# VectorE's attention heads in free row groups, with a re-ordered start, in a transformer block on one core

## The chip, the cores and the metric

The kernel runs on one core of one Trainium2 chip, whose engines each work through an instruction stream of their own: TensorE (PE, matmuls), ScalarE (ACT, activations), VectorE (DVE), GpSimd (POOL) and SyncE (SP, which issues the DMA transfers). The metric is the device time of one execution in microseconds (us). Three runs of the kernel before took 921.13, 921.31 and 921.42 us; the median is 921.31 us.

## The reference

The block is a pre-layernorm attention block followed by a gated MLP, for 2048 tokens of width 640, with 32 heads of width 20 and an MLP width of 1728. All inputs are bf16.

```python
x   = A_x                                          # [1, 2048, 640]
qkv = (layernorm(x) @ wqkv) -> q, k, v             # 32 heads of width 20
p   = softmax(q @ k^T * 20 ** -0.5)                # per head, 2048 x 2048
h   = x + (p @ v, heads side by side) @ wo
n   = layernorm(h)
h2  = h + (gelu_tanh(n @ w_gate) * (n @ w_up)) @ w_down
```

## The kernel before

**Who computes the exponentials.** The scores of 32 heads are 32 x 2048 x 2048 numbers, and every one needs an exp. The scores are computed transposed, in tiles of 128 keys by up to 512 queries for one head. Heads are packed by four (index `j` = 0 to 3): head `j` of a group `g` has its 20 rows of K and Q in partitions 32j to 32j+20 (`kt_all`, `qt_all`), so four heads use four different row groups of the PE array, and matmuls of different `j` can run beside each other. Most tiles get their exp on ACT (`activation` with Exp, out of PSUM into the ring `pts`/`pts2`). A part gets it on DVE, by an evacuation to int16 (line 870) and six arithmetic instructions per two or four tiles (`d_exp`).

**Chunks, slots, units.** The queries are cut in seven chunks (`CHUNKS`: 512, 512, 256, 256, 256, 128, 128). A chunk has slots; a slot is one to four head groups, in all 32 slots, and its sum over keys is gathered in PSUM bank 6. Within a slot some quads (a quad is one block of keys for four heads) are taken out for DVE (`D_QUADS`), and their single tiles are listed in `dq` with the place in the stream from which each is due (lines 793 to 811). The other tiles are walked in order and cut in units (lines 813 to 832): 3 tiles, then 2 tiles, and so on, because a unit's scores stand in PSUM banks 0 to 2 or 3 to 4 (chunk 1 uses 3 to 5 as well). One ACT instruction does the exp of a whole unit: 128x1536 or 128x1024. A unit can carry one tile for DVE (`xd`), which is the next in `dq` when it is due. `unit()` issues the scores of its own tiles (line 935), then the tile for DVE by an operation of its own into bank 5 or 7, then the exp, then the products with V (`pv_op`) of quads that are complete. The plan has 703 units, 1776 tiles for ACT and 272 tiles for DVE.

**A planner writes the order.** Every operation is recorded with an engine, an assumed duration, a priority, its reads and writes and its PSUM banks. `Sched.schedule` (line 120) plays this out as a list schedule: each engine takes the ready operation of the best priority, and the result is one fixed order per engine, with semaphore waits. All engines then run their lists in order. A changed duration in a call of `op` thus changes no work, but the order of everything. The priorities are `P_QK` 0 (scores, exps), `P_PV` 1, `P_PRO` 1.5 (the start), `P_EPI` 2, `P_LN` 2.5, `P_BG` 3 (projections and MLP in the background). Nearly all recorded lambdas have line 354 (`I`), so groups of the profile are told apart by their tiles.

**The start.** x is loaded by four DMAs (`x0` to `x3`, 4 tiles of 128 rows each). The layernorm statistics are computed by DVE (`ln_stats`), for `x1` by ACT (`act_stats`); ACT takes the square roots (`sd`), DVE the reciprocals (`rs`) and applies them (L354, `rege<-rege,mu,rs`). PE transposes the rows (line 592), and ACT or DVE (`T_DVE`) evacuates them into `xnT` (lines 598, 601). K and Q of tile 0 (four heads plus) are projected in blocks `c` of 512 tokens (`proj_qk`, matmuls in line 649) and evacuated by ACT (line 682); SP copies the rows to their partitions. `kd` holds the largest |k| of each row over all keys; with `sel0` and |q| a matmul (line 770) gives an upper bound of each query's scores, which is added as one more row of Q (line 774) and keeps the exp in range. Only then can the first scores start. Ones in column 20 of each head of `v_all` give the softmax sums.

**K tiles 1 to 4** are projected during chunk 0 (`proj_k`, `proj_q`, `q_bound`), evacuated by DVE (line 685) and go through HBM (`k_rows`, `q_rows`, `bounds`) to their partitions.

**Behind a chunk** `epilogue` divides by the sums and `post` does the output projection, the layernorm, and the MLP in the background of the next chunk (lines 1107, 1153, 1164). ACT's Gelu and Sqrt need another table than Exp: in the stream, a batch of Gelu (on DVE's copies of the gate values, line 1142) stands between two table loads. In `post` of the last chunk, the tail, ACT takes Gelu straight from PSUM (line 1129).

Of the kernel before, what the change touches and what calls it, by code (L numbers as in the profile page):

```python
# [307 lines left out]
SIZES = (512, 512, 256, 256, 256, 128, 128)  # L308
CHUNKS = tuple((sum(SIZES[:i]), n) for i, n in enumerate(SIZES))
# [14 lines left out]
D_FIRST, D_PART = 2, 0.75  # L324
# [5 lines left out]
P_QK, P_PV, P_PRO, P_EPI, P_LN, P_BG = 0, 1, 1.5, 2, 2.5, 3  # L330


def bass_sequential_preLN__mha_block__glu_gated_geglu__prompt_kernel(
# [12 lines left out]
    with ExitStack() as es:  # L346
# [133 lines left out]
        op("act", I("activation", nm[:, 0:1], zer[:, 0:2].bitcast(FP32), ACT.Sqrt), 1.5, P_QK, reads=["zer"], writes=["nm0"])  # L480
# [4 lines left out]
        op("dve", I("memset", f32(kt_all[:, 1:4, :]), ones2), 2.9, P_QK, writes=["kf0"])  # L485
# [16 lines left out]
        for j in range(4):  # L502
# [3 lines left out]
              base=0, pattern=[[-1, 128]], channel_multiplier=1), "identf")  # L506
        for g in range(0, NG, 2):
            cst(I("memset", f32(qt_all[:, 3, g:g + 2, :]), 0.0), "qf3%d" % g, 512)
        pvb0 = Bank(6)
        op("dve", I("memset", PS[:, 512 * 6:512 * 7], 0.0), 0.6, P_QK, acq=[pvb0], rel=[pvb0])  # L510
        op("dve", I("memset", v_all[:, :, :, DH:DH + 1], 1.0), 0.6, P_QK, writes=["vones"])
# [19 lines left out]
        e_ops = []  # L531
        C_POOL, T_POOL, T_DVE = 0.9, (), (13, 15)
# [11 lines left out]
        def ln_rsqrt(t0, n, prio, table=False, sqrt=False):  # L544
# [15 lines left out]
            if sqrt:  # L560
                op("act", I("activation", sd16[:, t0:t0 + n], sd16[:, t0:t0 + n], ACT.Sqrt), 0.2, 1, reads=[ks], writes=[ks])
                v(I("reciprocal", y, sd16[:, t0:t0 + n]), [ks], rk)
                return
# [15 lines left out]
        def ln_apply(eng, src, dst, dkey, t, rkeys, prio, first=False):  # L579
# [5 lines left out]
            return op(eng, fn, 0.82 if eng == "act" else C_POOL if eng == POOL else c_dve(D, 0.46), prio,  # L585
# [43 lines left out]
        for t0 in (0, 4, 8, 12):  # L629
# [6 lines left out]
            for t in range(t0, t0 + 4):  # L636
                e_ops.append(ln_apply(POOL if t in T_POOL else "dve", x_sb[:, t, :], xn_p[:, t % 4, :], ("xnp", t % 4), t, [f"x{t // 4}"], P_PRO,
# [9 lines left out]
        def chain(bk, key, n, steps, reads, prio, acq=True, after=()):  # L647
            for k, (l, r) in enumerate(steps):
                yield op("pe", lambda eng, l=l, r=r, k=k: eng.matmul(  # L649
                    bank(bk, n), l, r, start=(k == 0), stop=(k == len(steps) - 1)),  # L650
                    c_mm(n), prio, mode="full", util=n / 2400.0, reads=reads, writes=[key], acq=[bk] if (k == 0 and acq) else [],
# [17 lines left out]
        def proj_qk(col, t, c, dst, dkey, banks, prio, evac, after=(), peak=None):  # L669
# [9 lines left out]
            if peak and c == 3:  # L679
                after = (top(lambda: bank(bk), key),)  # L680
# [7 lines left out]
            if peak and c < 3:  # L688
                w_readers.append(top(lambda: dst, dkey))

        def proj_k(t, banks, prio, evac="dve"):
            for c in range(4):
                src = k_un[t % 2][:, 512 * c:512 * c + 512]
                proj_qk(D, t, c, src, ("ku", t % 2, c), banks, prio, evac, after=e_ops if t == 1 else (), peak=t == 0)
# [8 lines left out]
                if t and c == 3:  # L703
                    c0 = 0
# [552 lines left out]
```

## Time and profile before

| | before |
|---|---|
| median of 3 runs | 921.31 us |
| the profiled execution, its own time | 921.06 us |
| its span, first to last instruction | 919.1 us |
| ACT busy | 877.0 us (95%) |
| PE busy | 846.4 us (92%) |
| DVE busy | 794.5 us (86%) |
| exps on ACT | 370 of 128x1536, 333 of 128x1024 |
| first exp starts | 35.42 us |
| last exp ends | 883.5 us |

Times in the profile are counted from the start of the span. "Busy" is the union of the recorded instructions of an engine; instructions of one engine overlap in their records, since the next starts while the last one drains, so the step from start to start tells more than the recorded length. "Idle" in brackets names who released an instruction after a wait. The granted TensorE clock is 1.000 in this execution.

### The profile page before, as it was taken

Reading aid. Unit: us, or ns where it says so; the run is one execution under the profiler, and the core shown is the slowest. Engines: PE = TensorE matmul, PEld = TensorE weight load, DVE = VectorE, ACT = ScalarE, POOL = GpSimd, SP = SyncE. Lnnn points to the kernel's source line nnn. Section 1 sums busy time; section 2 is a strip of 40 time slices with the busy share of each in tenths; the row PEclk is TensorE's granted clock in tenths of the full one; section 3 lists DMA queues with packets and bytes.
Section 4 is the critical chain, followed back from the end, with each engine's and each line's share of the span. In section 5 each row is a group of like instructions: output and inputs, shape, how many; then the busy total and the mean of one; then the engine's idle time right before and its main releaser. Section 6 shows DMA issues by size and latency. Waiting matters only on the chain.

```text
span 919.1 us, 23058 instructions
## 1 busy us (share of the span) xinstructions
PE 846.4 (92%) x10159; PEld 355.6 (39%) x10159; DVE 794.5 (86%) x1456; ACT 877.0 (95%) x787; POOL 42.1 (5%) x121
## 2 busy tenths in 40 slices
PE   3999999999898987989998998999999999999998
PEld 1432323222232222223343333344444445666577
DVE  7779999999799996988888999899999988878763
ACT  6899999999999999999999999999999999999961
POOL 5000000000001000000001000000202000100200
PEclk9999999999999999999999999999999999999999
DMA  7211021234701000000111000010110001000000
GB/s 257 82 33 44 19 55 50 80 77 89 274 1 30 1 1 2 1 1 16 44 30 31 2 2 1 1 17 30 23 37 2 16 9 38 17 17 24 9 17 16
DMA packets 39516, 34.36 MB, mean 37 GB/s; under 512 B 19436, under 2 KB 36936, under 8 KB 39416
## 3 DMA queue, kind: packets, MB, share of 16 engines
q1 hardware_dynamic: 39416, 32.89, 12.9%
q8 instruction: 80, 1.31, 0.6%
q14 instruction: 20, 0.16, 0.1%
HBM read 20.12 MB, written 8.09 MB: 31 GB/s over the span
## 4 chain that ended last, share of the span: by engine, by line
ACT 62%; PE 27%; DVE 11%; issue 1%; DVEq 0%
ACT pts L354 39%; ACT rege L354 22%; PE ps L935 8%; PE ps L1107 6%; PE ps L354 5%; DVE qt_all L354 4%; PE ps L1164 4%; PE ps L649 3%; DVE qt_all L870 2%; ACT L354 1%; DVE rege L870 1%; DVE stats L354 1%; PE ps L592 1%; PE ps L1030 1%; DVE rege L354 1%
## 5 line engine op out<-in xcount | busy, mean ns | idle before, releaser
L354 ACT ACTIVATE pts<-ps 128x1536 bf16<-128x1536 f32 (+1 forms) x471 | 559.3, 1318 | 3.5 <-PE ps L935 1.5
L935 PE MATMUL ps<-qt_all,kt_all 32*128 32x256 bf16 (+2 forms) x3584 | 320.8, 288 | 37.7 <-ACT pts L354 22.3
L354 ACT ACTIVATE rege<-ps 128x1536 bf16<-128x1536 f32 (+1 forms) x232 | 285.2, 1317 | 2.6 <-PE ps L354 2.0
L935 PEld LDWEIGHTS ps<-qt_all,kt_all 32*128 32x128 bf16 x3584 | 104.3, 92 | 259.0 <-ACT pts L354 135.1
L354 DVE TENSOR_TENSOR qt_all<-qt_all 128x2048 f16<-128x2048 f16 (+3 forms) x186 | 174.9, 940 | 2.2
L1107 PE MATMUL ps<-rege,regw 128*128 128x256 bf16 (+2 forms) x980 | 160.9, 290 | 9.9 <-ACT rege L354 3.4
L354 PE MATMUL ps<-pts,v_all 128*21 128x256 bf16 (+2 forms) x2080 | 122.6, 290 | 0.0
L870 DVE TENSOR_SCALAR qt_all<-ps 128x512 int16<-128x512 f32 x128 | 87.6, 685 | 27.5 <-PE ps L935 27.0
L870 DVE TENSOR_SCALAR rege<-ps 128x512 int16<-128x512 f32 x128 | 87.5, 684 | 15.6 <-PE ps L935 13.9
L1107 PEld LDWEIGHTS ps<-rege,regw 128*128 128x128 bf16 x980 | 71.9, 97 | 70.6 <-issue 28.7
L354 PE MATMUL ps<-rege,v_all 128*21 128x256 bf16 (+2 forms) x1204 | 94.9, 295 | 0.3
L649 PE MATMUL ps<-regw 128*128 128x512 bf16 (+1 forms) x360 | 87.9, 353 | 1.1 <-DVE rege L870 0.6
L354 DVE TENSOR_SCALAR qt_all<-qt_all 128x1024 f16<-128x1024 int16 (+2 forms) x153 | 84.9, 559 | 1.8
L1164 PE MATMUL ps<-regw,rege 128*128 128x320 bf16 x448 | 79.0, 301 | 1.7 <-DVE rege L1153 0.6
L354 DVE TENSOR_TENSOR rege<-rege 128x1024 f16<-128x1024 f16 (+4 forms) x102 | 66.0, 657 | 1.0
L354 PE MATMUL ps<-kt_all,zer 128*32 128x512 bf16 x736 | 60.6, 384 | 0.0
L354 PEld LDWEIGHTS ps<-pts,v_all 128*21 128x21 bf16 x2080 | 44.9, 91 | 33.3 <-issue 29.3
L354 DVE TENSOR_SCALAR rege<-rege 128x1024 int16<-128x1024 int16 (+2 forms) x117 | 50.2, 447 | 1.1
L1164 PEld LDWEIGHTS ps<-regw,rege 128*128 128x128 bf16 x448 | 37.3, 97 | 33.9 <-issue 16.2
L1153 DVE TENSOR_TENSOR rege<-rege,ps 128x512 bf16<-128x512 bf16 (+1 forms) x53 | 35.7, 676 | 14.3 <-PE ps L1107 14.1
L649 PEld LDWEIGHTS ps<-regw 128*128 128x128 bf16 x360 | 29.2, 98 | 46.8 <-issue 24.8
L354 PEld LDWEIGHTS ps<-rege,v_all 128*21 128x21 bf16 x1204 | 32.4, 91 | 24.7 <-issue 16.8
(106 smaller groups left out, 564.9 us busy)
## 6 DMA issues: line engine op xcount, KB each, us to landing
rege<-in_A_x_dram SPq DMA_DIRECT2D x6, 640.0 KB, 5.2
q_rows<-regw SPq DMA_DIRECT2D x20, 128.0 KB, 1.7
out_dram<-rege SPq DMA_DIRECT2D x16, 160.0 KB, 1.8
regw<-in_B_w_gate_dram SPq DMA_DIRECT2D x1, 2160.0 KB, 12.8
regw<-in_B_w_up_dram SPq DMA_DIRECT2D x1, 2160.0 KB, 17.8
regw<-in_B_w_down_dram SPq DMA_DIRECT2D x1, 2080.0 KB, 22.9
kt_all<-k_rows SPq DMA_DIRECT2D x12, 160.0 KB
qt_all<-q_rows SPq DMA_DIRECT2D x12, 160.0 KB
```

What stands on the lines that cost most here:

```text
L354: return lambda eng: getattr(eng, method)(*args, **kwargs)
L592: op("pe", lambda eng, a=a: eng.transpose(bank16(bk, D)[:, 128 * a:128 * a + 128], src[:, a * 128:(a + 1) * 128], ident[:]), 0.055, prio, ...
L649: yield op("pe", lambda eng, l=l, r=r, k=k: eng.matmul(bank(bk, n), l, r, start=(k == 0), stop=(k == len(steps) - 1)), c_mm(n), prio, mode ...
L870: d_ops.append(op("dve", lambda eng: eng.tensor_scalar(v[:, 512 * h:512 * h + 512], bank(b), EXP_MUL, -32000.0, ALU.mult, ALU.max), c_dve( ...
L935: return lambda eng: eng.matmul(out()[:, kk * nq:(kk + 1) * nq], kt_all[32 * j:32 * j + 32, g, kt * 128:(kt + 1) * 128], qt_all[32 * j:32 ...
L1030: op("pe", lambda eng, tt=tt: eng.transpose(bank(b2)[:, tt * 128:(tt + 1) * 128], osb[:, s, tt * 128:(tt + 1) * 128], identf[:]), c_mm(128 ...
L1107: op("pe", lambda eng, a=a, f=f, fi=fi: eng.matmul(bank(bk)[:, fi * nq:(fi + 1) * nq], w[:, a, F0[f]:F0[f] + 128], hnT[:, a, 128 * tb:128 ...
L1153: hdone.append(op("dve", lambda eng, bu=bu, fv=fv, w=w: eng.tensor_tensor(fv, fv, bank(bu, w), ALU.mult), c_dve(w), p, reads=[ku] + hkeys( ...
L1164: op("pe", lambda eng, f=f, o=o, hf=hf, bk=bk: eng.matmul(bank(bk, 320), ha_f[:, o:o + 128], wd[:, f, hf * 320:(hf + 1) * 320], start=(f = ...
```

## The change

1. The memset of V's ones goes from DVE's list to POOL's, behind `identf`.
2. At the start, evacuations of K and Q wait for the three square roots that are still to come (`sqrts`); tile 11's transposes go to DVE's evacuations (`T_DVE`); the four DMAs of Q's tile 0 come ahead of K's by a better priority; `cold` adds 0.1 us to the planned duration of early matmuls; two more planned durations are raised.
3. The largest |k| of K tiles 1 to 4 is found block by block with one `tensor_reduce` each, as for tile 0, in place of a mask, three maxima and a reduce over the whole tile. For tiles 1 to 4, Q is projected ahead of K.
4. A unit's tile for DVE is picked from the next four in `dq`, of the same quad, so that its `j` is none of the unit's own. If none fits, the unit carries none. The planned duration of its scores is 0.01 us (0.21 where `j` is shared) and was 0.08 us.
5. Planned durations of scores and of products with V are 0.222 us per unit or quad (0.215, 0.218), and chunk 0's tiles for DVE are spread over 0.65 of a slot (`D_PART`, 0.75).
6. `BASE`, `SIX`, `P_LND`, `P_LNP`, `q_done` write out what was computed or fixed before, with the same values.

```diff
-D_FIRST, D_PART = 2, 0.75
+D_FIRST, D_PART = 2, 0.65
...
-        op("dve", I("memset", f32(kt_all[:, 1:4, :]), ones2), 2.9, P_QK, writes=["kf0"])
+        op("dve", I("memset", f32(kt_all[:, 1:4, :]), ones2), 4.2, P_QK, writes=["kf0"])
...
+        cst(I("memset", v_all[:, :, :, DH:DH + 1], 1.0), "vones", 512)
         for g in range(0, NG, 2):
             cst(I("memset", f32(qt_all[:, 3, g:g + 2, :]), 0.0), "qf3%d" % g, 512)
...
-        op("dve", I("memset", v_all[:, :, :, DH:DH + 1], 1.0), 0.6, P_QK, writes=["vones"])
...
-        C_POOL, T_POOL, T_DVE = 0.9, (), (13, 15)
+        T_DVE = (11, 13, 15)
...
+            cold = 0.1 if prio == P_PRO and not any(("xnT", tt) in reads for tt in range(4, NT)) else 0.0
...
-                    c_mm(n), prio, mode="full", util=n / 2400.0, reads=reads, writes=[key], acq=[bk] if (k == 0 and acq) else [],
+                    c_mm(n) + cold, prio, mode="full", util=n / 2400.0, reads=reads, writes=[key], acq=[bk] if (k == 0 and acq) else [],
...
-            if peak and c == 3:
-                after = (top(lambda: bank(bk), key),)
+            if prio == P_PRO:
+                after = tuple(sqrts)
+            if peak and c == 3 and t == 0:
+                after += (top(lambda: bank(bk), key),)
...
-            if peak and c < 3:
+            if peak and (c < 3 or t):
                 w_readers.append(top(lambda: dst, dkey))
...
-                if t and c == 3:
-                    c0 = 0
-                    n = 2048
-                    w_readers.append(op("dve", I("tensor_scalar", ka[:, 512 * c0:512 * c + 512].bitcast(I16),
...
-            for n in (1024, 512, 256) if t else ():
-                op("dve", I("tensor_tensor", ka[:, 0:n], ka[:, 0:n], ka[:, n:2 * n], ALU.max), 0.066 + n * 0.00052, prio,
...
-                        [("qu", 0), "qtm0"], "qc", 2.2, prio)
+                        [("qu", 0), "qtm0"], "qc", 2.2, prio - 0.1)
...
-            if di < len(dq) and dq[di][0] <= i:
-                xd = dq[di][1]
-                di += 1
-            n = len(bs) - (1 if six and xd else 0)
+            n = len(bs)
+            if dq and dq[0][0] <= i:
+                n -= 1 if six else 0
+                js = [x[3] for x in tiles[i:i + n]]
+                q = dq[0][1][:3]
+                fit = [k for k in range(min(4, len(dq))) if dq[k][1][:3] == q and dq[k][1][3] not in js]
+                if fit:
+                    xd = dq.pop(fit[0])[1]
+                elif six:
+                    n += 1
...
-            qk = op("pe", fns, 0.215, P_QK, mode="row", util=0.0533 * len(al), reads=reads, writes=[("S", u), "qkseq"] + ([("SD", xd)] if six else []), acq=bks)
+            qk = op("pe", fns, 0.222, P_QK, mode="row", util=0.0533 * len(al), reads=reads, writes=[("S", u), "qkseq"] + ([("SD", xd)] if six else []), acq=bks)
...
-                qd = op("pe", [qk_mms(lambda: bank(bd), xd, kk) for kk in range(512 // CHUNKS[slots[xd[0]][0]][1])], 0.08,
+                qd = op("pe", [qk_mms(lambda: bank(bd), xd, kk) for kk in range(512 // CHUNKS[slots[xd[0]][0]][1])],
+                        0.21 if xd[3] in [x[3] for x in tl] else 0.01,
...
                     pr = P_EPI if t == 1 else P_BG
+                    proj_q(t, 0, BG0, pr)
                     proj_k(t, BG0, pr)
-                    proj_q(t, 0, BG0, pr)
```

## The prediction

> **What bounds the kernel.** I read the page first, then ScalarE's timeline, then all engines at the start, at the longest waits and in the tail. The page's busy row and its chain of waits:
>
> ```profile
> PE 846.4 (92%) x10159; PEld 355.6 (39%) x10159; DVE 794.5 (86%) x1456; ACT 877.0 (95%) x787; POOL 42.1 (5%) x121
> ACT 62%; PE 27%; DVE 11%; issue 1%; DVEq 0%
> L354 ACT ACTIVATE pts<-ps 128x1536 bf16<-128x1536 f32 (+1 forms) x471 | 559.3, 1318 | 3.5 <-PE ps L935 1.5 <-PE ps L354 1.4
> ```
>
> ACT carries the chain from 42 to 866 us, nearly all of it exps. The 370 wide exps step by 1.330 us at best and the 333 narrow ones by 0.903: 370 x 1.330 + 333 x 0.903 = 792.8 us. Their steps in the trace sum to 812.3. So 19.5 us of lateness lies between exps; 35.4 us lie before the first, 35.6 behind the last. The change can act on these three parts alone: as the two programs are built, both have 370 and 333 exps.
>
> **The start, before.** DVE and POOL, then ACT and DVE around the first K block:
>
> ```profile
> 2.76 3.98 POOL L354 MEMSET kt_all<- 128x1024 f32 x4
> 4.22 0.48 DVE L354 MEMSET ps<- 128x512 f32 x1
> 6.54 0.48 DVE L354 MEMSET v_all<- 128x512 bf16 x1 [1.84 <-issue]
> ...
> 20.91 0.60 ACT L682 ACTIVATE regw<-ps 128x512 bf16<-128x512 f32 x1 [2.41 <-PE ps L649]
> 21.41 0.38 ACT L354 ACTIVATE sd<-sd 128x4 bf16<-128x4 bf16 x3
> 22.18 0.60 ACT L682 ACTIVATE regw<-ps 128x512 bf16<-128x512 f32 x1 [0.39 <-PE ps L649]
> 22.67 0.76 ACT L788 ACTIVATE v_all<-ps 128x320 bf16<-128x320 f32 x2
> 23.90 6.07 ACT L598 ACTIVATE regw<-ps 128x640 bf16<-128x640 bf16 x10 [0.46 <-PE ps L592]
> 35.42 1.45 ACT L354 ACTIVATE pts<-ps 128x1536 bf16<-128x1536 f32 x1 [1.12 <-PE ps L935]
> ...
> 21.54 0.69 DVE L677 TENSOR_REDUCE kd<-regw 128x1 f32<-128x512 bf16 x1 [1.09 <-ACT regw L682]
> 22.14 0.23 DVE L354 RECIPROCAL rs<-sd 128x4 f32<-128x4 bf16 x2
> 22.83 2.94 DVE L354 TENSOR_SCALAR rege<-rege,mu,rs 128x640 bf16<-128x640 bf16 x8 [0.45 <-DVE rs L354]
> 31.69 0.68 DVE L677 TENSOR_REDUCE kd<-ps 128x1 f32<-128x512 f32 x1
> 32.28 0.69 DVE L685 CAST rege<-ps 128x512 bf16<-128x512 f32 x1
> ```
>
> The ones of V wait 1.84 us, until POOL's fourth memset is nearly over, and the first layernorm statistics stand behind them at 6.65, though x0 landed at 5.17. Later, DVE's reciprocals stand behind a 0.69 us reduce; so normalised rows come at 22.83, and ten evacuations of 0.6 us keep ACT until 29.97.
>
> **Term 1, the start.** (a) Without the memset, statistics start at 5.2 and end near 19.3 (20.45 before; one wait for x2 eats 0.5). This alone buys little: PE's four V matmuls wait for `wv`, landed at 16.96, so K's first block starts at 18.2 rather than 18.56. (b) The square roots run in ACT's idle 2.41 us, reciprocals come before the reduce, and rows 4 and on are normalised from about 20. Then PE is late: K and Q's first blocks are ten matmuls, 0.427 us each until about 21.1 and 0.213 after, so they end at 21.8, and in the new order transposes follow at once, where ten V matmuls stood. Q's evacuation ends near 22.4, and ACT's transposed rows run from there. (c) They are nine, DVE taking tile 11: 22.4 + 9 x 0.6 = 27.8, against 29.97. (d) Behind them ACT's list has K, V, K where K, K stood: +0.4. (e) The 0.69 us cast is out of the bound's chain: -0.6. Sum: -2.2 + 0.4 - 0.6 = -2.4; I take **-2.3**, the first exp at 33.1. Ends: -1.0 (only c and part of e) and -3.5 (b and c by the rows' earlier readiness).
>
> Moved past by this: SP issues Q's four DMAs (0.75 us each) after two of K's, so K's block 0 lands up to 3.0 us later than 25.94; the first scores want it at 33. POOL's four `qt_all` memsets and the tiny `mu` operations move back by V's memset (0.48 on DVE; POOL's 128x512 took 0.54); POOL's next customer there is `mu` at 19.8, and it was idle from 15.5. Cover gone, that is 0.5 us.
>
> The Trainium skill (SBUF — State Buffer, "Who interferes with whom") speaks of a lock: a DVE operation in a 2-port mode and a POOL operation exclude each other for a whole instruction, while on trn2 it names no memset among such operations. By it the ones on POOL may now hold up a layernorm `tensor_scalar` for one memset, and the 1.84 us would be no lock and might stay. In the rows, such operations took 0.61, 0.51 and 0.61 us beside POOL's memsets at 13.2 to 15.6 and about 0.37 a step alone; by the rule's strict reading (a) is gone, and the sum moves by 0.4 us at most, since (b) to (e) don't rest on it.
>
> **Term 2, heads in free row groups.** I walked the planning loop of both versions. Before, 171 of the 272 tiles for DVE share `j` with a tile of their unit; after, none does. What sharing costs:
>
> ```profile
> 140.50 0.61 PE L935 MATMUL ps<-qt_all,kt_all 32*128 32x512 bf16 x3
> 141.80 0.39 PE L935 MATMUL ps<-qt_all,kt_all 32*128 32x512 bf16 x3
> ...
> 169.32 2.37 ACT L354 ACTIVATE pts<-ps 128x1536 bf16<-128x1536 f32 x2 [1.35 <-PE ps L354]
> ```
>
> Three matmuls with a shared `j` took 0.61 us, three without 0.39. So PE gets 171 x 0.22 = 38 us back, out of 781 us busy between 35 and 870 (of 835). PE isn't the bound, so the worth is what ACT no longer waits. Nearly all lateness comes at a wide exp behind a narrow one, when PE has only 0.9 us. Wide exps whose preceding unit carried a shared tile start 63 ns late on average (112 of them); behind a free tile 24 (78), behind none 21 (175). Taking 63 to 24 gives 112 x 39 ns = **-4.4 us**. Ends: 0 (other work fills PE's queue at the same points) and -7.1 (all 112 x 63).
>
> **Term 3, ends of slots.** Three waits over 0.7 us stand out: 0.8 at 142, 1.5 at 168, 1.5 at 694, each just ahead of an `osb` copy, a slot's end, where the products of DVE's last tiles bunch in PE's list and hold up the ring that exps write. Two are in chunk 0, where the last DVE tile was 4 to 5 units from the end; with `D_PART` and the new picks it is 7 to 9 in all slots but slot 5 (4). I take half of these two: **-1.2**. Ends: -3.8 and, as new waits may come in an order that is new everywhere, +3.
>
> **Term 4, the tail.**
>
> ```profile
> 883.53 1.28 ACT L354 ACT_TABLE_LOAD   x1
> 887.84 0.70 ACT L598 ACTIVATE rege<-ps 128x640 bf16<-128x640 bf16 x1 [2.81 <-PE ps L592]
> 892.77 0.21 ACT L354 ACTIVATE sd<-sd 128x1 bf16<-128x1 bf16 x1 [4.22 <-DVE sd L354]
> 912.32 3.98 PE L1164 MATMUL ps<-regw,rege 128*128 128x320 bf16 x28 [0.59 <-DVE rege L1132]
> ```
>
> The new list has two more table loads (16, was 14): chunk 5's Gelu now comes ahead of O's evacuation. ACT then has 1.28 + 0.2 + 1.28 + 1.7 = 4.5 us to do where 4.3 us lay between 883.53 and 887.84; the next load of 1.28 falls in the 4.22 us wait. So +0.2 of 2.6. PE, which is busy throughout, has 30.7 us of columns behind the last scores (31.0 before), and one wait more for DVE (0.6, as the row at 912.32). I take **+0.3**; ends -0.5 and +2.6.
>
> **Edits at nothing.** The block-wise reduces: 4 x 0.68 + 0.15 = 2.88 us against 0.68 + 0.68 + 0.41 + 0.28 + 0.41 = 2.46 per K tile, +1.7 us in all, on a DVE with 25 us idle between 35 and 275. Their cover is the 8 us between the landing of K and bounds for groups 1 and 2 (52.6) and first use (about 60); Q ahead of K takes some 2 of it, the start moves both. Without cover each late us costs one. The written-out constants keep their values.
>
> **Sum.** -2.3 - 4.4 - 1.2 + 0.3 = -7.6. Against the profiled execution's 921.06 that is 913.5; the median is 0.25 above it, so **913.7 us**.
>
> **Rivals.**
> - *PE's relief is not ACT's.* The late exps after shared tiles may owe their wait to what stands behind them in PE's list; PE's busy 93% speaks for it, the 63 against 24 against it. Term 2 is 0: 918.1. Chance 0.14.
> - *DVE tiles bunch (other side).* Chunk 0's eight tiles per slot need 8 x 0.6 + 4 x 3.33 = 18.1 us of DVE, now due within 0.65 x 26 = 16.9 us (19.5 before), and DVE was busy 93.3 of 100 us from 100 to 200. If DVE falls behind, PE's in-order list stops at bank 5 or 7 or at the slot's last products, as at 169.32, by 1.35 us. It decides from six such new waits on (8.1 against 7.6); one at each of the 20 slots in chunks 0 to 3 and term 3 gone: 913.7 + 1.2 + 13.5 = 928. The five tile buffers and the 9 us left to each slot's end speak against it. Chance 0.13.
> - *The change does nothing where it counts:* the start gains 1.0 by its low end, the tail loses that; 921.3. Chance 0.04.
>
> **Numbers.** The likeliest has 0.69; its own range adds its terms' likelier ends: -3.5 - 6 - 2 - 0.3 gives 909.5, -1 - 2 + 0 + 1.5 gives 919.8. To leave out no more than 2 in 10, I take 908.5 to 920.0, which also holds the first rival. 0.2% (1.8 us) is about what a measurement here tells from no change. Faster 0.83 (likeliest and first rival), same 0.04, slower 0.13.
>
> **What would show it.** The first exp near 33.1, its statistics from 5.2 on; scores of unit and tile for DVE in one 0.39 us; exps' lateness near 14 us and no 63 against 24; no wait over 0.7 us before 243; the tail 35 to 36 us. Wrong: new waits of ACT for PE L354 or L936 at slots' ends, or oT's evacuation over 5 us behind the last exp.

## The result and the profile after

The changed kernel took 922.38 us (median of 22 executions, 920.48 to 926.52), the kernel before 921.22 (920.35 to 921.89, also 22). The ratio is 1.0016, 95% interval 1.0010 to 1.0022: within 0.2% of no change, on its slow side, where 913.7 was forecast.

One thing is needed to read these numbers. The kernel before is tight; the changed one spreads, and the spread goes with the granted TensorE clock: its mean was 1.000 in 2 of the 22 executions (920.48 and 920.67), 0.998 in 10 (median 921.91), 0.996 in 6, 0.994 in 3 (median 924.06) and 0.989 in 1 (926.52). The profiled execution took 921.85 us at 0.998. The kernel before has such executions too, though fewer and cheaper: of the 84 that were timed beside the experiments, 62 had 1.000 (median 921.06), 16 had 0.998 (921.54) and 6 had 0.996 (922.02). So the changed kernel's two executions at the full clock lie about 0.5 us below the 921.06 of the kernel before (two are few), and the 1.2 us by which it is slower in the median go with the clock. The other 7 us that miss the forecast are missing at the full clock too.

The page of the changed kernel, the lines that answer to those shown of before:

```profile
PE 837.6 (91%) x10145; PEld 353.1 (38%) x10145; DVE 798.5 (87%) x1456; ACT 878.4 (95%) x788; POOL 38.3 (4%) x122
ACT 67%; PE 24%; DVE 8%; DMA 1%; issue 1%; POOL 1%
L357 ACT ACTIVATE pts<-ps 128x1024 bf16<-128x1024 f32 (+1 forms) x472 | 563.7, 1354 | 8.0 <-PE ps L936 4.8
L936 PE MATMUL ps<-qt_all,kt_all 32*128 32x256 bf16 (+2 forms) x3584 | 306.7, 289 | 46.6 <-ACT pts L357 26.6
```

TensorE was relieved (846.4 to 837.6 us busy), ScalarE is bound as before, and the idle time ahead of its exps rose from 3.5 to 8.0 us in the costliest group. "Lateness" is counted below as in the prediction: the step from one exp to the next, less 1.330 us (wide) or 0.903 (narrow), without the five steps that hold a Gelu. So counted, the kernel before has 18.47 us of it, where the prediction has 19.5. "Rests" in the table is what the last exp takes beyond its best step.

| profiled execution, us | before | after | difference | forecast |
|---|---|---|---|---|
| first exp | 35.42 | 32.75 | -2.67 | -2.3 |
| lateness to 100 us | 1.29 | 3.19 | +1.90 | |
| lateness 100 to 200 | 3.42 | 6.12 | +2.70 | |
| lateness 200 to 500 | 5.62 | 3.81 | -1.81 | |
| lateness 500 to 700 | 5.43 | 5.42 | 0.0 | |
| lateness behind 700 | 2.70 | 4.36 | +1.66 | |
| all lateness | 18.47 | 22.90 | +4.43 | -5.6 |
| five Gelu gaps and rests | 36.82 | 36.86 | 0.0 | |
| behind the last exp | 35.59 | 34.58 | -1.01 | +0.3 |
| span | 919.10 | 919.89 | +0.79 | -7.6 |

The start and the tail did what was forecast or better. The lateness went the other way, and three places in the trace carry it.

**The seventh exp.** ScalarE's timeline around the first exps, changed kernel:

```profile
31.36 1.28 ACT L357 ACT_TABLE_LOAD   x1
32.75 4.62 ACT L357 ACTIVATE pts<-ps 128x1536 bf16<-128x1536 f32 x4
37.23 2.40 ACT L357 ACTIVATE rege<-ps 128x1536 bf16<-128x1536 f32 x2
42.27 3.71 ACT L357 ACTIVATE pts<-ps 128x1536 bf16<-128x1536 f32 x3 [2.63 <-PE ps L357]
```

and the kernel before, ScalarE, then TensorE:

```profile
42.36 4.62 ACT L354 ACTIVATE pts<-ps 128x1536 bf16<-128x1536 f32 x4
...
41.38 0.61 PE L354 MATMUL ps<-pts,v_all 128*21 128x512 bf16 x8
```

Six exps start 2.67 us earlier, and the seventh starts at 42.27 against 42.36. It writes slots of the ring `pts` that the first products with V must have read; these are TensorE's matmuls at 41.61 (41.38 before). What they stand behind, VectorE and TensorE of the changed kernel:

```profile
37.40 0.68 DVE L871 TENSOR_SCALAR rege<-ps 128x512 int16<-128x512 f32 x1
37.99 0.68 DVE L691 CAST rege<-ps 128x512 bf16<-128x512 f32 x1
38.94 1.29 DVE L871 TENSOR_SCALAR rege<-ps 128x512 int16<-128x512 f32 x2 [0.26 <-PE ps L936]
40.14 0.68 DVE L681 TENSOR_REDUCE kd<-rege 128x1 f32<-128x512 bf16 x1
40.73 0.42 DVE L357 TENSOR_SCALAR rege<-rege 128x1024 int16<-128x1024 int16 x1
41.07 0.49 DVE L783 CAST v_all<-ps 128x320 bf16<-128x320 f32 x1
...
41.30 0.39 PE L742 MATMUL ps<-regw,sel 128*32 128x512 bf16 x1
41.61 0.61 PE L357 MATMUL ps<-pts,v_all 128*21 128x512 bf16 x8
```

VectorE works, with one gap of 0.26 us, on K tile 1 (L691, L681) and on the first tiles of slot 0 (L871), and its cast of a V tile (L783) comes at 41.07. The products start 0.54 us behind it.

**The bounds of group 4.** ScalarE, SP's queue, then TensorE, changed kernel:

```profile
138.00 1.54 ACT L357 ACTIVATE pts<-ps 128x1536 bf16<-128x1536 f32 x1
143.37 3.28 ACT L357 ACTIVATE pts<-ps 128x1024 bf16<-128x1024 f32 x3 [3.83 <-PE ps L936]
...
130.82 1.43 SPq L357 DMA_DIRECT2D kt_all<-k_rows  x4
136.50 0.32 SPq L357 DMA_DIRECT2D bounds<-regw  x1
137.97 0.57 SPq L357 DMA_DIRECT2D qt_all<-bounds  x1
...
140.50 0.61 PE L357 MATMUL ps<-rege,v_all 128*21 128x512 bf16 x8
...
142.94 0.60 PE L936 MATMUL ps<-qt_all,kt_all 32*128 32x512 bf16 x5
```

SP's queue, kernel before:

```profile
129.29 0.33 SPq L354 DMA_DIRECT2D bounds<-regw  x1
...
130.76 0.57 SPq L354 DMA_DIRECT2D qt_all<-bounds  x1
```

The bounds are written 7.2 us later than before, and slot 4 needs them at 139: lateness 4.04 us. Not all of this is the transfer's: the bounds have landed by 139.82 in the trace, but slot 4's scores start at 142.94, as TensorE's fixed list has products with V, projections and transposes in between.

**A dip of the clock.** Stretches of the changed kernel (from and to in us; length; busy time and count of PE, PEld, DVE, ACT, POOL; granted clock; DMA share; GB/s):

```profile
664.00:666.00 2.00, 1.51 (x33) 0.91 (x30) 2.00 (x4) 2.00 (x3) 0.30 (x2) 1.00 0.00 0
666.00:669.00 3.00, 1.81 (x18) 0.64 (x15) 3.00 (x5) 3.00 (x4) 0.00 (x0) 1.00 0.02 5
669.00:671.00 2.00, 1.89 (x32) 0.93 (x32) 2.00 (x7) 2.00 (x3) 0.00 (x0) 0.53 0.00 0
671.00:672.50 1.50, 1.50 (x26) 0.42 (x18) 0.85 (x2) 0.64 (x2) 0.00 (x0) 0.50 0.20 40
672.50:675.00 2.50, 2.50 (x41) 1.04 (x33) 1.53 (x4) 2.19 (x3) 0.00 (x0) 0.99 0.54 107
```

Behind a stretch in which TensorE had little but scores of 32 rows, the clock was 0.50 for 3.4 us (669.1 to 672.5), and the two exps at its end were 1.08 and 0.43 us late. In the profiled execution of the kernel before it was 1.00 until the last exp.

### The profile page after: what moved, and what is told of

Its sections match the earlier page's. It is cut to its first block, busy times and chain, and to the rows that moved or that the text cites. A ratio compares the mean times of both kernels' runs of the same rounds, so it can differ in the third digit from the quotient of the medians.

```text
span 919.9 us, 23052 instructions
## 1 busy us (share of the span) xinstructions
PE 837.6 (91%) x10145; PEld 353.1 (38%) x10145; DVE 798.5 (87%) x1456; ACT 878.4 (95%) x788; POOL 38.3 (4%) x122
## 3 DMA queue, kind: packets, MB, share of 16 engines
q8 instruction: 79, 1.29, 0.6%
## 4 chain that ended last, share of the span: by engine, by line
ACT 67%; PE 24%; DVE 8%; DMA 1%; issue 1%; POOL 1%
ACT pts L357 42%; ACT rege L357 23%; PE ps L936 7%; PE ps L1107 5%; PE ps L357 4%; PE ps L1164 4%; PE ps L653 3%; DVE qt_all L357 2%; ACT L357 1%; DVE stats L357 1%; DVE qt_all L871 1%; DVE rege L357 1%; DVE rege L871 1%; PE ps L1029 1%; DVE rege L1142 1%
## 5 line engine op out<-in xcount | busy, mean ns | idle before, releaser
L357 ACT ACTIVATE pts<-ps 128x1024 bf16<-128x1024 f32 (+1 forms) x472 | 563.7, 1354 | 8.0 <-PE ps L936 4.8
L936 PE MATMUL ps<-qt_all,kt_all 32*128 32x256 bf16 (+2 forms) x3584 | 306.7, 289 | 46.6 <-ACT pts L357 26.6
L357 ACT ACTIVATE rege<-ps 128x1024 bf16<-128x1024 f32 (+1 forms) x231 | 289.4, 1361 | 2.5 <-PE ps L936 2.2
L936 PEld LDWEIGHTS ps<-qt_all,kt_all 32*128 32x128 bf16 x3584 | 100.1, 92 | 271.1 <-ACT pts L357 142.5
L1107 PE MATMUL ps<-rege,regw 128*128 128x256 bf16 (+2 forms) x980 | 157.9, 290 | 9.0 <-ACT rege L357 3.1
L871 DVE TENSOR_SCALAR qt_all<-ps 128x512 int16<-128x512 f32 x128 | 87.7, 687 | 15.4 <-PE ps L936 14.5
L871 DVE TENSOR_SCALAR rege<-ps 128x512 int16<-128x512 f32 x128 | 87.4, 686 | 13.5 <-PE ps L936 12.4
L357 DVE TENSOR_TENSOR rege<-rege 128x1024 f16<-128x1024 f16 (+1 forms) x90 | 61.5, 683 | 0.8
L357 PEld LDWEIGHTS ps<-pts,v_all 128*21 128x21 bf16 x2070 | 45.1, 91 | 31.5 <-issue 27.8
L357 DVE TENSOR_SCALAR rege<-rege 128x1024 int16<-128x1024 int16 (+2 forms) x115 | 48.2, 440 | 0.7
```

What stands on the lines that cost most here:

```text
L357: return lambda eng: getattr(eng, method)(*args, **kwargs)
L871: d_ops.append(op("dve", lambda eng: eng.tensor_scalar(v[:, 512 * h:512 * h + 512], bank(b), EXP_MUL, -32000.0, ALU.mult, ALU.max), c_dve( ...
L936: return lambda eng: eng.matmul(out()[:, kk * nq:(kk + 1) * nq], kt_all[32 * j:32 * j + 32, g, kt * 128:(kt + 1) * 128], qt_all[32 * j:32 ...
L1107: op("pe", lambda eng, a=a, f=f, fi=fi: eng.matmul(bank(bk)[:, fi * nq:(fi + 1) * nq], w[:, a, F0[f]:F0[f] + 128], hnT[:, a, 128 * tb:128 ...
```

## The experiments

Each was timed against the kernel before; ratios are to its executions on the same chip (medians of 921.03 to 921.28 us on the four chips used). A table at the end of this section sets the main ones side by side.

**1. The start alone.** The changed kernel with all else undone:

```diff
-D_FIRST, D_PART = 2, 0.65
+D_FIRST, D_PART = 2, 0.75
...
+            if di < len(dq) and dq[di][0] <= i:
+                xd = dq[di][1]
+                di += 1
...
+                    proj_k(t, BG0, pr)
                     proj_q(t, 0, BG0, pr)
-                    proj_k(t, BG0, pr)
```

(and the old chain for K's maxima, and the old durations 0.218, 0.215 and 0.08).

> The kernel before with the new start alone: ones of V by GpSimd, square roots ahead of the evacuations, Q's transfers first, tile 11 to VectorE. K's maxima of tiles 1 to 4 by the old chain, K ahead of Q, heads picked as before, planner's durations and D_PART as before. Theory 1, the prediction's first term stands on its own: first exp near 32.8 and no wait of ScalarE behind it, so 921.2 - 2.5 = 918.7 (918.2 to 919.2). Theory 2, the gain is lost before the 8th exp, because the seventh needs ring slots that the first products with V free, and those come no earlier: first exp near 32.8, a wait of 2 to 3 us at the 7th exp near 42, 920.5 to 921.7. The granted clock should stay at 1.000 under both, as the order behind 60 us is close to the one before.

Measured: 921.88 us, ratio 1.0011 (1.0002 to 1.0021). ScalarE's timeline of it:

```profile
32.80 4.62 ACT L357 ACTIVATE pts<-ps 128x1536 bf16<-128x1536 f32 x4
37.28 2.40 ACT L357 ACTIVATE rege<-ps 128x1536 bf16<-128x1536 f32 x2
42.50 3.71 ACT L357 ACTIVATE pts<-ps 128x1536 bf16<-128x1536 f32 x3 [2.82 <-PE ps L357]
```

The second theory holds: first exp at 32.80, seventh at 42.50, nothing gained. The clock, which both theories wanted at 1.000, was so in 6 of 10 executions (median of these 921.69).

**2. The heads alone.** The kernel before with the pick, the durations and `D_PART` of the change:

```diff
-D_FIRST, D_PART = 2, 0.75
+D_FIRST, D_PART = 2, 0.65
...
-            if di < len(dq) and dq[di][0] <= i:
...
+            n = len(bs)
+            if dq and dq[0][0] <= i:
```

> The kernel before with the free row groups alone: the new pick of VectorE's tiles, the three written-out durations of the planner and D_PART 0.65; the start, the order of K and Q and K's maxima as before. Theory 1, the prediction's second and third terms: exps behind what were shared tiles are no longer late and two waits at slots' ends are shorter, 921.2 - 5.6 = 915.6 (913.5 to 918). Theory 2, the order of VectorE's and TensorE's lists in the first 200 us decides, and a free pick is worth little by itself: no wait of 4 us near 138, since K ahead of Q gives the bounds in time, but not over 2 us gained, 919 to 921.5. If TensorE's relief lets its granted clock dip here too, the clock is under 1.000 and the time 1 us above either for each dip of 3.4 us.

Measured: 921.69 us, 1.0014 (1.0001 to 1.0026). Lateness fell by 1.2 us (18.47 to 17.25): the waits at 143, 169 and 695 (3.85 together) went, and others came. Chunk 5's Gelu now stood ahead of the last exps, so the five Gelu gaps took 1.9 us more (38.6 against 36.7) while the tail stayed at 35.43. The second theory, 919 to 921.5, holds at the full clock (921.07 in the median of 6 executions); the other four, at 0.994 to 0.998, took 922.34 to 925.77.

**3. K ahead of Q again.**

```diff
+                    proj_k(t, BG0, pr)
                     proj_q(t, 0, BG0, pr)
-                    proj_k(t, BG0, pr)
```

> The changed kernel with one line undone: for the K tiles 1 to 4, K is projected before Q again. Theory, Q ahead of K makes K's bounds late: the 3.83 us wait of ScalarE near 138 (scores of group 4 behind bounds that landed at 139.8) goes, and 922.4 falls by 2.5 to 4, to 918.4 to 920. Rival, K's and Q's order only moves the wait, because VectorE is behind by as much whatever comes first: waits of 1 to 4 us somewhere from 100 to 200, 921 to 923. The wait at the 7th exp (2.6 us) stays under both, as nothing near 40 us changes but the two evacuations' order.

Measured: 922.73 us, 1.0027 (1.0009 to 1.0045). The place does what the theory says, ScalarE and SP's queue:

```profile
137.32 4.71 ACT L357 ACTIVATE pts<-ps 128x1536 bf16<-128x1536 f32 x4
141.79 2.50 ACT L357 ACTIVATE rege<-ps 128x1536 bf16<-128x1536 f32 x2
...
132.12 0.32 SPq L357 DMA_DIRECT2D bounds<-regw  x1
```

The bounds are written at 132.12 and not at 136.50, and the 3.83 us wait is gone. But lateness from 100 to 200 us fell only from 6.12 to 3.92, since waits of 1.48 at 168 and 0.81 at 194 came, the tail was 0.84 longer, and 1.9 us of Gelu moved ahead of the last exps. In time the rival was right.

**4. Zero matmuls ahead of scores**, eleven sets of four:

```diff
+                if e == "pe" and self.pad is not None and not live and o.tag and o.tag[0] == "S":
+                    while recent and recent[0][0] < t - PAD_WIN:
+                        recent.popleft()
+                    if sum(x for _, x in recent) < 0.35 * PAD_WIN and free["act"] > t + o.dur + .45:
+                        o.fns = [lambda eng, j=j, b=o.acq[0]: self.spad(eng, b, j) for j in range(4)] + o.fns
...
+        sc.spad = lambda eng, b, j: eng.matmul(PS[32 * j:32 * j + 32, 512 * b.b:512 * b.b + 512], zer[:], kt_all[:, 0, 0:512],
+                                               start=True, stop=True, tile_position=(0, 32 * j), skip_group_check=True)
```

> The changed kernel with eleven sets of four more zero matmuls, each ahead of a unit's scores into the bank that these overwrite, at places where the planner counts less than 0.35 of full matmul use over 3.4 us and nothing else fills TensorE (one is the stretch from 665.6 to 669.7); the order of everything else is the same. Theory, the dips of the granted clock that follow such stretches cost about 1 us each and explain why the changed kernel's runs spread from 920.5 (clock 1.000) to 926.5 (clock 0.989): clock 1.000 in all runs, spread under 0.5 us, median near 920.5 (920.2 to 921.0). Rival, the dips come from elsewhere or cost nothing on the path: clock 0.998 and lower as before, median 922.4 +- 0.7, or, if the added matmuls stand in the way of scores, 11 x 0.2 = 2.2 us more.

Measured: 922.27 us, 1.0017 (1.0007 to 1.0027). The clock was 1.000 in 6 of 10 executions, where it had been in 2 of 22, and the profile has no dip at 669. But executions at 1.000 took 921.27 to 922.44: above the theory's 920.2 to 921.0. The clock is the theory's and the median the rival's: dips became rarer and the time stayed.

**5. V's tiles 4 and 5 ahead of K tile 1.**

```diff
-            proj_v(kt, 0, (6, 7, 5), P_EPI if kt < 4 else P_BG, "act" if kt < 4 else "dve")
+            proj_v(kt, 0, (6, 7, 5), P_EPI if kt < 6 else P_BG, "act" if kt < 4 else "dve")
```

> The changed kernel with one line edited: V's key tiles 4 and 5 (first half of the heads) get the priority of tiles 0 to 3, ahead of K tile 1's background work. Theory 2a, the seventh exp waits because VectorE's casts of V stand behind K tile 1's casts and maxima and the first tiles for VectorE: the 2.63 us wait near 42 goes (under 0.5). As VectorE has the same work to do between 31 and 60 us, a part of it, 1 to 3 us, comes back as a wait near 50 to 56, where the products want V's later tiles. 921 to 922.5. Theory 2b, it is bank 6 or TensorE alone that is late there: the wait at 42 stays over 2 us. The prediction's view, that nothing but the first exp counts, expects no wait at either place and 919.7 or less. The wait near 142 may change, since the order behind 60 us is new.

Measured: 925.1 us, 1.0041 (1.0026 to 1.0056). ScalarE's timeline:

```profile
39.31 4.85 ACT L357 ACTIVATE pts<-ps 128x1536 bf16<-128x1536 f32 x4
...
51.16 1.02 ACT L357 ACTIVATE pts<-ps 128x1024 bf16<-128x1024 f32 x1 [1.14 <-PE ps L357]
...
55.53 2.37 ACT L357 ACTIVATE pts<-ps 128x1536 bf16<-128x1536 f32 x2 [1.08 <-PE ps L357]
```

Theory 2a: the wait at 42 is gone, and 1.32 + 1.21 us of lateness came back at 51 and 55.5. All its executions had dips of the clock (0.998 or less), and chunk 5's Gelu was ahead again, so the time was worse than expected.

**6. No quad for VectorE in slot 0**, on top of experiment 5:

```diff
-D_QUADS = (1,) + (2,) * 15 + (2, 2) + (3, 2) * 5 + (2, 2, 2, 2)
+D_QUADS = (0,) + (2,) * 15 + (2, 2) + (3, 2) * 5 + (2, 2, 2, 2)
```

> As the kernel before it (V's tiles 4 and 5 ahead), and slot 0 has no quad for VectorE: four heads' tiles go to ScalarE, which costs it 4 x 443 = 1.8 us of exps and spares VectorE 4 x 0.6 + 3.33 = 5.7 us between 35 and 45 us. Theory 2a, VectorE's backlog is what gives the start's gain back: no wait over 0.4 us before 80 us, that is 2.5 to 4 us less lateness by 80 us than in the changed kernel (2.9 us by then). If so, what the start gains is bounded by VectorE's work, not by ScalarE's. Theory 2b expects the wait unchanged with or without the quad. The whole time is no test here, as the last slots are cut anew: 920 to 925.

Measured: 926.5 us, 1.0064 (1.0049 to 1.0079); no wait over 0.45 us before 80. So with 5.7 us less work on VectorE, and in these runs only then, the start's gain passes 60 us: 0.58 us of lateness by then, against 0.55 before and 2.84 in the changed kernel. ScalarE pays for it with four more tiles to exp. (The whole time is lost further on: lateness 500 to 700 us was 10.1, and the tail 38.1.)

**7 and 8. Combined.** Experiment 7 is the changed kernel with K first, V's tiles 4 and 5 ahead and `D_PART` 0.70; experiment 8 has K first, the old chain for K's maxima, V's tiles 4 to 7 ahead and `D_PART` 0.65.

```diff
-D_FIRST, D_PART = 2, 0.65
+D_FIRST, D_PART = 2, 0.7
...
-            if peak and (c < 3 or t):
+            if peak and c < 3:
```

(the first pair is 7's, the second, the head of the old chain, is 8's.)

> The changed kernel with K ahead of Q again for K tiles 1 to 4, V's tiles 4 and 5 ahead, and D_PART 0.70. Theory: the start's gain and the slots' ends are lost to single waits that the order of VectorE's list sets, so without them 3 to 5 us appear: no wait of over 1.5 us before 300; the 2.6 us at 42 shrinks to about 1.3 at 50, and 143, 168 and 194 are gone; 917 to 919.5 (chunk 5's Gelu ahead of the last exps adds 1.9 us, as in the heads alone). Rival, every order of this list loses as much somewhere else: 920.5 to 922.5.

> The changed kernel with K ahead of Q, K's maxima of tiles 1 to 4 by the old chain, which costs VectorE 2.46 us per tile where the block-wise one costs 2.88, and V's tiles 4 to 7 ahead; D_PART stays 0.65. Same theory as for the combined kernel: one wait of 2 to 3 us near 55, none over 1 us from 60 to 300, chunk 5's Gelu in the tail; 916.5 to 919 at a granted clock of 1.000, and 1 us more for each dip of it, as the thin stretch ahead of 665 us is as in the changed kernel. Rival: 920.5 to 922.5.

Measured: 917.78 us, 0.9970 (0.9959 to 0.9982), and 917.54 us, 0.9964 (0.9951 to 0.9977), both within what the theory gave. In 7 the only wait over 0.5 us ahead of 500 is 1.23 at 51; lateness in all is 15.94 us. In 8 the wait is 2.96 at 55.7, so that the start's gain is gone by 60 us again (3.03 us of lateness by then); what 8 keeps is 3.7 us less lateness than the kernel before between 100 and 500 us, and a tail 1.0 shorter. No execution of 8 had a clock of 1.000; its dip:

```profile
660.00:663.00 3.00, 2.24 (x38) 1.12 (x34) 3.00 (x5) 3.00 (x4) 0.00 (x0) 1.00 0.00 0
663.00:664.90 1.90, 1.36 (x20) 0.59 (x22) 1.90 (x4) 1.90 (x3) 0.00 (x0) 0.99 0.00 0
664.90:668.40 3.50, 3.50 (x43) 1.19 (x37) 2.99 (x7) 2.74 (x3) 0.00 (x0) 0.52 0.26 52
```

**9. Experiment 8 with three sets of zero matmuls**, and **10. the changed kernel with the same three**, all three in the stretch ahead of 670:

```diff
+                if e == "pe" and self.pad is not None and not live and t > 640 and o.tag and o.tag[0] == "S":
...
+                    if sum(x for _, x in recent) < 0.30 * PAD_WIN and free["act"] > t + o.dur + .45:
```

> The kernel with K ahead of Q, K's old maxima and V's tiles 4 to 7 ahead (917.5), with three sets of four zero matmuls more, ahead of scores in the thin stretch from 661.5 to 664.9, behind which the granted clock was 0.50 from 664.9 to 668.4; the order of everything else is the same. Theory, the dip costs the 1.7 us of lateness at 667 to 669 and three sets cost 0.2 us each at most: clock 1.000 in most runs, 916.0 to 916.8. Rival, the dip's place is hidden or moves: 917.2 to 918.

> The changed kernel with the same three sets, ahead of scores between 665.6 and 669.7, and none of the other eight that were tried before. Theory, the dip costs 1.2 us in the median and what ate the gain of eleven sets was the other eight in front of scores: clock 1.000 in most runs, 920.6 to 921.4. Rival, the dips of the changed kernel's runs mostly lie elsewhere: 922 to 922.7 with clocks of 0.998 and less.

Measured: 916.47 us, 0.9951 (0.9939 to 0.9963), with a clock of 1.000 in 4 of 5; and 922.86 us, 1.0020 (1.0010 to 1.0030), with 1.000 in 5 of 12. Experiment 9 is the fastest kernel of this study: 4.8 us below the kernel before. There the dip behaved as the theory says: none near 665, and one at 430.8 in the profiled execution, which is the one at 0.998. In experiment 10 it did not: the profile has none at 669 but one at 839.8, and the executions at 1.000 took 921.29 to 922.13, not 920.6. The rival's half, dips elsewhere, is part of it; the rest stays open.

**11. The pick alone**, with the old durations and `D_PART`:

```diff
+                js = [x[3] for x in tiles[i:i + n]]
+                q = dq[0][1][:3]
+                fit = [k for k in range(min(4, len(dq))) if dq[k][1][:3] == q and dq[k][1][3] not in js]
```

> The kernel before with the free pick alone; the planner's durations and D_PART 0.75 as before. Theory 1 of the prediction, sharing costs ScalarE 39 ns for each of 112 exps: 917 or less, and no new wait. Theory 2, the relief is worth some 2 us, and single waits that the new order makes in chunk 0 can exceed it: the exps of chunk 1 are 2 to 2.5 us less late than before, as in the kernel with all three edits, but one or two waits of 1 to 4 us come between 135 and 200, and the time is 921 to 925.

Measured: 924.56 us, 1.0039 (1.0025 to 1.0054). New waits of 4.22 at 142, 1.01 at 171 and 1.73 at 198, from an edit that touches only which unit carries which tile for VectorE. Chunk 1 was 2.6 us less late (4.71 to 2.10), as the second theory has it.

**12. The ones of V by VectorE.**

```diff
-        cst(I("memset", v_all[:, :, :, DH:DH + 1], 1.0), "vones", 512)
...
+        op("dve", I("memset", v_all[:, :, :, DH:DH + 1], 1.0), 0.6, P_BG, writes=["vones"])
```

> The changed kernel with the ones of V written by VectorE again, right behind its memset of PSUM. If the 1.84 us that it waited there before is tied to the memsets of GpSimd, statistics start near 6.6 again and not at 5.07, and the normalising operation that took 2.04 us beside GpSimd's 2.37 us memset takes 0.4 to 0.6. Theory, neither is on the path, since K's first block waits for the weights until 17 to 18.3: first exp 32.5 to 33.0, as in the changed kernel. Rival, the later statistics are passed on: first exp 33.5 to 34.3. The order behind 60 us is new, so the 4 us wait near 143 may be another; the whole time, 920 to 923, is no test.

Measured: 922.21 us, 1.0010 (1.0001 to 1.0018). First exp at 32.64, as with GpSimd's memset. VectorE and POOL of this kernel:

```profile
6.54 0.48 DVE L357 MEMSET v_all<- 128x512 bf16 x1 [1.84 <-issue]
6.65 1.22 DVE L357 BATCH_NORM_STATS2 stats<-rege 128x6 f32<-128x320 bf16 x3
...
14.50 0.51 DVE L357 TENSOR_SCALAR rege<-rege,mu,rs 128x640 bf16<-128x640 bf16 x1
```

and of the changed kernel:

```profile
5.07 1.28 DVE L357 BATCH_NORM_STATS2 stats<-rege 128x6 f32<-128x320 bf16 x3 [0.37 <-DMA rege<-in_A_x_dram]
...
12.80 2.04 DVE L357 TENSOR_SCALAR rege<-rege,mu,rs 128x640 bf16<-128x640 bf16 x1
...
12.29 2.37 POOL L357 MEMSET v_all<- 128x512 bf16 x1
```

So the memset's move is worth nothing by itself, as step (a) had it: 1.6 us of earlier statistics end in front of the same weights.

**13 and 14. The pick in chunk 1 alone, and everywhere else alone.**

```diff
+                free = slots[tiles[i][0]][0] == 1
+                fit = [k for k in range(min(4, len(dq))) if dq[k][1][:3] == q and dq[k][1][3] not in js] if free else [0]
```

(14 has `!= 1`.)

> The kernel before, with the free pick for units of chunk 1 only (243 to 457 us); chunk 0 keeps its order, so nothing may change before 243. Theory, all of the relief is in chunk 1: its exps are 2 to 3 us less late than before (4.7 us there), the first exp of chunk 2 comes at 454.1 to 455.1 (457.1 before), and what the later order makes of it is open: 918 to 921. The prediction's pooled price, 39 ns for each wide exp behind a shared tile, gives 36 x 39 ns = 1.4 us: 455.7.

> The kernel before, with the free pick everywhere but in chunk 1. Theory: outside chunk 1 the tile's matmuls follow the unit's own as a separate operation, so a shared row group doesn't hold up the scores that ScalarE waits for: mean lateness of wide exps behind a unit with a tile stays at 35 to 60 ns in chunks 0 and 2 to 6 (42 before, shared and free together), chunk 1's stay as before near 60, and waits of 4 us at 142 and 1 to 2 us at 171 and 197 come from the new order in chunk 0: 923 to 930, with the tail cut anew. The prediction's pooled price: 76 x 39 ns = 3.0 us less, 918 to 919.

Measured: 922.78 us, 1.0022 (1.0002 to 1.0042), and 936.97 us, 1.0174 (1.0159 to 1.0190). In 13 chunk 1 was 2.1 us late where it was 4.7, and chunk 2 began 418.86 us behind the first exp, 421.70 before: -2.84, twice the pooled price. The gain was then lost: a 1.32 us wait at 533, and a tail of 37.6. In 14 chunk 1's wide exps behind shared tiles were 87 ns late, as before, and those behind a tile in other chunks 57 ns (39 before, shared and free together), so nothing was gained; one more chunk's Gelu moved behind the last exp, and the tail was 49.7 us. What the scores kept TensorE busy, in the kernel before, in 13 and in 14:

```profile
L935 PE MATMUL ps<-qt_all,kt_all 32*128 32x256 bf16 (+2 forms) x3584 | 320.8, 288 | 37.7 <-ACT pts L354 22.3
L942 PE MATMUL ps<-qt_all,kt_all 32*128 32x256 bf16 (+2 forms) x3584 | 313.2, 288 | 48.8 <-ACT pts L354 28.4
L942 PE MATMUL ps<-qt_all,kt_all 32*128 32x256 bf16 (+2 forms) x3584 | 320.1, 289 | 51.6 <-ACT pts L354 30.4
```

Freeing chunk 1's 37 shared tiles took 7.6 us off, 0.21 each; freeing the other 134 took 0.7 us off in all (this profile has a dip of 3.4 us, which makes some of its matmuls longer).

**15. The start alone, with V's tile 4 ahead of K tile 1.**

```diff
-            proj_v(kt, 0, (6, 7, 5), P_EPI if kt < 4 else P_BG, "act" if kt < 4 else "dve")
+            proj_v(kt, 0, (6, 7, 5), P_EPI if kt < 5 else P_BG, "act" if kt < 4 else "dve")
```

> The kernel with the new start alone (921.9), and V's key tile 4 ahead of K tile 1. Theory 2a: the 2.98 us wait at 42.5 goes, some 1.5 us of it comes back near 47, and 1.0 to 1.5 us of the start's gain show: 920.2 to 921.0 at a granted clock of 1.000. Rival, the same total in another place: 921.5 to 922.3.

Measured: 922.44 us, 1.0009 (1.0000 to 1.0018); at a clock of 1.000, 921.15 to 921.55. The wait at 42.5 went, 1.69 at 48, 0.67 at 55 and 0.8 more at 140 came. That is near the rival (921.5 to 922.3) and not theory 2a (920.2 to 921.0 at the full clock).

| kernel | first exp | lateness | waits over 0.8 us ahead of 300 | tail | median |
|---|---|---|---|---|---|
| before | 35.42 | 18.5 | 0.81, 1.53 | 35.6 | 921.2 |
| changed | 32.75 | 22.9 | 2.80, 4.04 | 34.6 | 922.4 |
| 1 start | 32.80 | 21.6 | 2.98, 0.81, 1.53 | 35.6 | 921.9 |
| 2 heads | 34.41 | 17.3 | 0.86 | 35.4 | 921.7 |
| 3 K first | 32.57 | 20.1 | 2.86, 1.48, 0.81 | 35.4 | 922.7 |
| 5 V 4, 5 first | 32.59 | 21.4 | 1.32, 1.21, 1.37 | 35.4 | 925.1 |
| 7 combined | 32.55 | 15.9 | 1.23 | 35.4 | 917.8 |
| 8 combined | 32.55 | 18.5 | 2.96 | 34.6 | 917.5 |
| 9 combined | 33.04 | 19.0 | 2.96 | 34.6 | 916.5 |

First exp, lateness and tail are of the one profiled execution (in 9 one with a dip that cost 1.46 us).

## Why the prediction was wrong

In the profiled executions the forecast of -7.6 us was missed by 8.4: lateness by 10.0, less 0.4 that the start and 1.3 that the tail did better.

**Term 1, the start (-2.3): right in size, wrong in worth.** ScalarE's nine rows ran from 22.29 to 27.76 (22.4 to 27.8 forecast), the first exp came at 32.75 (33.1). Over all profiles the unchanged starts lie at 34.41 to 35.42 (five, mean 34.83) and the new ones at 32.55 to 33.04 (twelve, mean 32.68): -2.15. The step that failed is to take the 35.4 us ahead of the first exp as a part by itself, each us of which counts. The prediction's own reading lets ACT carry the chain only "from 42 to 866 us". Up to there the chain runs through VectorE and the first products with V, six exps behind the first, and these did not move (41.38 before, 41.61 after). In place of -2.3, lateness to 100 us rose by 1.90, which left 0.8 of the 2.67. Experiments 1, 5 and 6 show it: the wait comes with the start alone, moves when V's casts move, and went only when VectorE had 5.7 us less to do.

**Term 2, free row groups (-4.4): the mechanism was right in chunk 1, and the size was a mean over unlike things.** Wide exps behind a unit with a tile for VectorE, mean lateness (count), waits over 0.7 us left out:

| | before, shared | before, free | after, free |
|---|---|---|---|
| chunk 1 | 94 ns (36) | 22 ns (28) | 23 ns (46) |
| other chunks | 49 ns (76) | 25 ns (50) | 49 ns (113) |

In chunk 1 a tile for VectorE stands in the unit's own group of matmuls (`six` in `unit()`; it is not an operation of its own there), so ScalarE waits for its row group; elsewhere its matmuls come behind the unit's, so that a shared row group delays the tile and not the unit. The split is shown; that this is its reason is argued from the program. TensorE's own relief was mis-sized too: 38 us were forecast, 0.22 for each of 171 shared tiles, and the scores' busy time fell by 14.1 (320.8 to 306.7), 8 of them in chunk 1. With the pick alone, the 0.22 holds for chunk 1's 37 tiles and not for the other 134 (experiments 13 and 14). The step that failed is the one price, 39 ns, for all 112 exps: the 63 against 24 of the prediction mixed these, and what it left, 24 ns for a free tile, was chosen by the old pick and did not hold for the new one. Chunk 1 paid 2.4 us (4.71 to 2.27), in experiment 13 2.6; the other chunks nothing (experiment 14).

**Term 3, ends of slots (-1.2).** The waits at 168 and 694 went as forecast, 3.0 us. But the stated end, new waits "in an order that is new everywhere", came as 4.04 us at 143, which is more than its +3, and a dip at 669. That one wait has a cause that stands among the **edits at nothing**: I covered Q ahead of K for groups 1 and 2 by the 8 us at 52.6 to 60, said that without cover each late us costs one, and left K tiles 2 to 4 unread. Tile 3, which brings group 4, had no cover; experiment 3 shows that K's and Q's order made this wait. How much the block-wise maxima add was not separated: 8 undid them together with other edits.

**Term 4, the tail (+0.3).** It was 1.0 shorter. The two more table loads cost nothing that shows: the five profiles with 16 loads have tails of 34.6, and of the twelve with 14 nine have 35.4 to 35.9, and experiments 13, 6 and 14 have 37.6, 38.1 and 49.7.

**Left out altogether: the clock.** The prediction gave TensorE's relief only an upside. The changed kernel had dips in 20 of 22 executions; by their medians the first 0.002 of mean clock, one dip, is 1.3 us (920.6 to 921.9). Of the 16 profiles of changed versions ten show dips ahead of the last exp, twelve in all, each of 3.4 or 6.8 us, at eight places; at the end of eleven of them exps are 1.0 to 1.8 us late. The Trainium skill (TensorE: Matmul & The Clock Gate, "The HAM clock gate") speaks of a window of 3413 ns without work behind which the clock is halved. The length fits these rows; the condition doesn't, since TensorE was busy 1.81 of 3.00 us ahead of the dip, with gaps of 0.57 us at most, though with scores of 32 rows; over all twelve dips it was busy 53 to 75% of the 3.4 us ahead, and no gap was over 0.84 us. That it is TensorE's relief that brings the dips isn't shown: experiments 1 and 15 have the old heads, and their clock was under 1.000 in 4 and 7 of 10 executions.

**The rivals.** "PE's relief is not ACT's" had the right reading for six of seven chunks but a time (918.1) that still counted the start. "Tiles bunch" had the right sign and the wrong mechanism: no tile for VectorE blocked a slot's end; VectorE's work for K and V came late. (Its 13.5 us are ten waits of 1.35; one at each of 20 slots is 27, and chunks 0 to 3 have 24.) "The change does nothing where it counts" came nearest in time (921.3, chance 0.04), by luck: it had the start and the tail cancel, and both gained, while lateness took the gain.

**What stays open.** Why experiment 10's executions without a dip (921.3 to 922.1) are slower than the changed kernel's two (920.5, 920.7); two are few. And which matmuls count against the dip was not tried.

## What to carry to other kernels

A gain ahead of the first instruction of the bound engine is kept only if the resource that it needs some steps later, here ring slots freed by another engine, comes earlier too: follow the chain behind the point that moves, not only up to it. Before a mean over groups of instructions is used as a price, split it by how these are issued; here one chunk of seven held all of it. Where a list planner orders all engines, an edit can bring new waits of 1 to 4 us anywhere, so a term smaller than those is worth forecasting only together with the new list's supply of each tile, read tile by tile; and with the causes known, four edits together (V's casts ahead, K ahead of Q, the old chain for K's maxima, zero matmuls in a thin stretch) turned +0.16% into -0.49%. No single one of the first, second and last did so alone (experiments 5, 3, 4 and 10), and the third was not run alone.

## What the runs showed of the hardware

- A memset by GpSimd of 128x512 bf16 elements, 21 apart, took 2.37 us, VectorE's 0.48; a VectorE `tensor_scalar` that began inside it took 2.04 us and ended 0.18 us behind it, against 0.51 without (experiment 12). The ten other kernels with GpSimd's memset have 2.42 to 2.43 and 1.76 to 1.77 us. The prediction set a rule of the Trainium skill (SBUF — State Buffer, "Who interferes with whom": a lock for a whole instruction) against three rows of 0.5 to 0.6 us; this row is on the rule's side, and it cost nothing here.
- VectorE's memset waited 1.84 us in all six kernels that have it, with POOL's memsets of `kt_all` running; the profile names no releaser.
- The granted clock goes to 0.50 for 3.4 us or twice that, although TensorE was busy 53 to 75% of the 3.4 us ahead, and not in every execution.
